# Attention stage of a fused attention and expert kernel: doubled result buffers, spread finish, earlier score groups, reordered start

## The chip, the cores and the metric

One core of a Trainium2 chip runs the program. The metric is device time in microseconds (us) of one execution; the kernel before takes 804.73 us, the median of 3 runs from 804.46 to 804.74. TensorE (PE) multiplies, VectorE (DVE), ScalarE (ACT) and GpSimd (POOL) work on tiles, SyncE (SP) issues transfers. Each engine works through its own instructions in the order in which the program has them.

## The reference

The computation is bucketed attention, then a gated product, then routed experts. The change touches the attention and the first of the gated products:

```python
q_bits = (np.einsum('bhsd,dk->bhsk', q, proj) > 0)     # 6 bits a row, k_bits likewise
mask = q_bucket[:, :, :, None] == k_bucket[:, :, None, :]
scores = np.where(mask, q @ k.T / sqrt(64), -1e9)      # 2 batches, 8 heads, 768 rows, 64 columns
attn = softmax(scores) ;  x = attn @ v                 # x: 1536 tokens x 512
x = (x @ w_a * (x @ w_b)) @ w_out                      # 512 -> 1536 -> 512, w in 64 bit
out = gate * relu(x @ w1[e]) @ w2[e]                   # one of 8 experts a token
```

## The kernel before

The attention works on eight pairs of heads (`i`). A pair has six **units** `u`, three a head, and a unit has two tiles of 128 query rows. All is in one loop over `u` from 0 to 49, in which each unit mixes the steps of several others:

- `scores(u, t)` (L161 to L172): four products into one of two score banks `st` (pool `ps_s`, two buffers). Half of them read swapped copies `qs`, `ks` of the transposed `q`, `k`, which SyncE makes (L127, L129).
- `rowmax` (L177) on VectorE, `expo` (L183) on ScalarE, which frees the score bank and sums; `recip` (L187), `normal` (L192 to L196) on GpSimd scales the exponentials; `turn` (L203) on VectorE transposes 32-blocks of unit `u - 2` into `et`.
- `pv` (L212): the product with `v`, 12 of a head's 24 blocks in a unit with `u % 3` of 0 or 1, into the four banks `pvb`. I call this a **product block**.
- in a unit with `u % 3 == 2` the four banks are read out and used for a later pair. `epilogue` (L230) copies them to `xp` and `co` on ScalarE. Then, where `u % 6 == 5` (a **turn unit**), `turned` (L107, L121) transposes the raw `q`, `k` of the pair after next, and where `u % 6 == 2` (a **sign unit**), `signs` (L139 to L152) makes the bucket codes `qf`, `kf` of the next pair (`sk` on the way).
- the **finish** of a pair, `xp + co` (L234, GpSimd), its high part `xh` (L238, ScalarE) and the rest `xl` (L242, GpSimd), stands at the ends of three units, `u % 6` of 5, 0 and 1. `xp` and `co` have one buffer each, so the `epilogue` of the next pair in the sign unit behind it writes the tiles that the finish reads.

The caller passes `hook`, with which steps of other work are placed at points of a unit: the weight splits (`load_first` for `w_a`, `w_b`, `w_out`: DVE steps L393, L396, L401, L415, ACT L409, L420, POOL L404, L421) by the table `places` and the list `tail`, and `fill`, which takes the first 16 half products of the gated stage (`gated_products`, L490, six matmuls each, copy `a` L498, product L502, cast L503) into units 41, 44, 47 to 49 and behind the loop. Behind the attention stands the gated stage, which begins with `yp` (L516).

Of the kernel before, what the change touches and what calls it, by code (L numbers as in the profile page):

```python
# [25 lines left out]
class Kernel:  # L26
# [37 lines left out]
    def attention(self, xh, xl, pools, hook):  # L64
# [9 lines left out]
        for tag, shape, dt, n in (  # L74
            ("et", [128, NC * S], F32, 2), ("e", [128, S], F32, 6), ("vr", [128, NC * 256], F32, 2), ("raw", [128, 2 * S], F32, 2),
            ("q", [128, S], F32, 2), ("qs", [128, S], F32, 2), ("k", [128, S], F32, 2), ("ks", [128, H2], F32, 2),
            ("xp", [128, S], F32, 1), ("co", [128, S], F32, 1), ("qf", [128, S], BF16, 2), ("kf", [128, S], BF16, 2), ("sk", [128, H2], BF16, 1),
        ):
            sb.tile(shape, dt, tag=tag, name=tag, bufs=n)
        raw, Q, QS, K, KS, QF, KF, VR = {}, {}, {}, {}, {}, {}, {}, {}  # L80

        def load(i, qs=(nc.sync, nc.sync)):
            b, hp = pairs[i]
            t = raw[i] = sb.tile([128, 2, NC, 2, D], F32, tag="raw", name="raw", bufs=2)
# [48 lines left out]
        def signs(i, n):  # L133
# [15 lines left out]
            def out():  # L149
                nc.scalar.activation(sk, p[:, 0, :H2], AF.Sign, bias=self.bias, scale=2.0 ** 100)  # L150
                for j in range(2):
                    nc.gpsimd.tensor_scalar(KF[i][:, j], sk, self.fac[:, j:j + 1], None, ALU.mult)  # L152
# [69 lines left out]
        def place(i, n, j, cs):  # L222
            if i not in XP:
                XP[i] = [sb.tile([128, S], F32, tag=t, name=t, bufs=1) for t in ("xp", "co")]
# [24 lines left out]
        hook(-1, 0)  # L249
        load(1)  # L250
        load_v(0)
        load_v(1)
# [9 lines left out]
        signs(0, 1)()  # L262
        signs(0, 0)()

        for u in range(NU + 2):
# [3 lines left out]
            done = (u - 11) // 6 if u >= 11 else -1  # L269
            fin = (u - 11) % 6  # L270
            if act:
                scores(u, 0)
                rowmax(u, 0)
            if s == 2 and u >= 8:
                for n in range(2):
                    epilogue((u - 8) // 3, n)
            if tr:
                turn(w, 0)
            if act:
                scores(u, 1)  # L280
                expo(u, 0)
            if last:
                recip(u - 1)
                normal(u - 1)
            hook(u, 3)
# [4 lines left out]
            preps = []  # L290
            if s == 2:
                n = (u + 7) // 6 if r == 5 else i + 1
                if u < NU and n < len(pairs):
                    preps = [(turned if r == 5 else signs)(n, x) for x in (1, 0)]
            elif u >= 6:
                pv((u - 6) // 3, range(12 * s, 12 * s + 12))
            if u == 0:
                n = 1
                preps = [turned(1, x) for x in (1, 0)]
            hook(u, 0)  # L300
            args = (nc.scalar,) if r in (5, 0) else ()
# [906 lines left out]
```

## Time and profile before

| | us |
|---|---|
| median of 3 runs | 804.73 |
| the profiled execution, its own time | 800.47 |
| its span on the core | 798.6 |
| TensorE busy | 727.9 (91%) |
| VectorE, GpSimd, ScalarE busy | 468.8, 458.8, 343.7 |

The page gives one execution. A share of busy time is a mean over stages with different limits: the attention stage fills the first 300 us or so of the span, and the rest is nearly all TensorE. What a change in the attention is worth is read from the waits of that stage and from the granted clock of its stretches (1.00 is 2.4 GHz, 0.5 is 1.2 GHz).

### The profile page before, as it was taken

The page shows a single profiled execution, that of the slowest core. Times are in us where ns is not written, and L with a number is a line of the kernel's source. Part 1 is how long each engine was busy: PE and PEld are TensorE (multiplying, and loading weights), DVE is VectorE, ACT ScalarE, POOL GpSimd, SP SyncE. Part 2 cuts the span into 40 slices and gives each one's busy share as a digit, 9 for nine tenths or more (in the row PEclk, how much of TensorE's full clock was granted, in tenths as well). Part 3 has the DMA queues.
Part 4 walks back from the last instruction along what each step waited for, and adds up shares of the span by engine and source line. Part 5 has one row for each costly group of instructions (what it writes and reads, how often), then busy time and mean ns, then how long its engine had stood idle before and what let it go on. Part 6 is the DMA issues. An engine that isn't in the chain of part 4 may idle for free.

```text
span 798.6 us, 16431 instructions
## 1 busy us (share of the span) xinstructions
PE 727.9 (91%) x6832; PEld 602.6 (75%) x6832; DVE 468.8 (59%) x679; ACT 343.7 (43%) x609; POOL 458.8 (57%) x468
## 2 busy tenths in 40 slices
PE   4788687798788789999999999999999999999996
PEld 3345354454456578999999999999999888899985
DVE  1499697786764826465465654643564665656551
ACT  1466466575653523421222212223353655555551
POOL 1387777787865654636356363555351575666651
PEclk9799999899997999999999999999999999999999
DMA  9433453542413131312113111144343376666620
GB/s 215 94 79 93 117 123 88 119 97 55 110 41 94 41 107 54 106 33 74 54 55 105 44 62 53 53 149 156 93 133 116 118 255 227 220 217 217 223 76 22
DMA packets 67485, 87.62 MB, mean 110 GB/s; under 512 B 28739, under 2 KB 40003, under 8 KB 67408
## 3 DMA queue, kind: packets, MB, share of 16 engines
q1 hardware_dynamic: 63200, 78.81, 34.3%
q0 software_dynamic: 2560, 7.34, 2.4%
q8 instruction: 54, 0.88, 0.5%
q10 hardware_dynamic: 1648, 0.39, 0.3%
q14 instruction: 23, 0.19, 0.1%
HBM read 75.52 MB, written 7.34 MB: 104 GB/s over the span
## 4 chain that ended last, share of the span: by engine, by line
PE 72%; POOL 8%; ACT 7%; DVE 5%; issue 4%; DMA 2%; SPq 1%; POOLq 0%; ACTq 0%; DVEq 0%
PE ab L490 23%; PE yp L516 12%; PE op L833 10%; PE hp L783 9%; PE st L170 3%; PE pv L212 3%; POOL e L196 3%; ACT e L183 3%; DVE nm L177 2%; PE pv L490 2%; POOL xl L242 2%; DVE et L203 2%; PE pv L139 2%; PE hr L801 1%; ACT co L230 1%
## 5 line engine op out<-in xcount | busy, mean ns | idle before, releaser
L490 PE MATMUL ab<-xh,w 128*128 128x384 f32 x704 | 185.7, 338 | 0.0
L177 DVE TENSOR_REDUCE nm<-st 128x1 f32<-128x768 f32 x96 | 90.7, 945 | 65.8 <-PE st L172 65.7
L490 PEld LDWEIGHTS ab<-xh,w 128*128 128x128 f32 x704 | 127.7, 188 | 0.8
L490 PE MATMUL ab<-xl,w 128*128 128x384 f32 x352 | 118.3, 336 | 0.0
L504 POOL TENSOR_TENSOR g<-a,g 128x384 fp32r<-128x384 f32 x48 | 50.0, 1042 | 114.1 <-ACT g L503 107.8
L739 POOL TENSOR_TENSOR w<-raw,w 128x1024 fp32r<-128x1024 f32 x36 | 88.1, 2450 | 36.7 <-ACT w L738 35.7
L183 ACT ACTIVATE e<-st,nm 128x768 f32<-128x768 f32 x96 | 86.2, 898 | 46.4 <-DVE nm L177 40.5
L516 PE MATMUL yp<-w,g 128*128 128x512 f32 x432 | 103.3, 391 | 0.8 <-DVE xp L335 0.8
L170 PE MATMUL st<-ks,qs 64*128 64x384 f32 x192 | 89.4, 547 | 15.4 <-DMA qs<-q 8.3
L196 POOL TENSOR_SCALAR e<-e,s,mc 128x768 f32<-128x768 f32 x96 | 96.5, 1012 | 5.3
L170 PE MATMUL st<-k,q 64*128 64x384 f32 x192 | 88.7, 543 | 10.7 <-ACT e L183 10.7
L203 DVE STREAM_TRANSPOSE et<-e 128x768 f32<-128x768 f32 x96 | 92.6, 965 | 0.0
L516 PEld LDWEIGHTS yp<-w,g 128*128 128x128 f32 x432 | 80.3, 188 | 16.3 <-PE yp L516 1.2
L833 PE MATMUL op<-w,hth 128*128 128x512 f32 x256 | 81.7, 400 | 0.0
L783 PE MATMUL hp<-xgh,w 128*128 128x256 f32 x448 | 80.6, 281 | 0.0
L212 PE MATMUL pv<-et,vr 32*64 32x192 f32 x3072 | 72.6, 331 | 4.5 <-ACT co L230 3.8
L212 PEld LDWEIGHTS pv<-et,vr 32*64 32x64 f32 x3072 | 61.4, 133 | 19.1 <-issue 7.3
L503 ACT CAST g<-a 128x384 fp32r<-128x384 f32 x48 | 24.7, 515 | 115.0 <-DVE a L502 115.0
L739 DVE TENSOR_TENSOR w<-raw,w 128x1024 fp32r<-128x1024 f32 x28 | 64.6, 2306 | 14.6 <-ACT w L738 14.3
L783 PEld LDWEIGHTS hp<-xgh,w 128*128 128x128 f32 x448 | 69.2, 188 | 0.3
L738 ACT CAST w<-raw 128x1024 fp32r<-128x1024 f32 x64 | 66.1, 1044 | 3.5 <-PE yp L516 3.5
L490 PEld LDWEIGHTS ab<-xl,w 128*128 128x128 f32 x352 | 66.2, 188 | 0.8
(189 smaller groups left out, 1217.5 us busy)
## 6 DMA issues: line engine op xcount, KB each, us to landing
raw<-in_moe_w_dram SPq DMA_DIRECT2D x32, 1024.0 KB, 5.7
vr<-in_v_dram SPq DMA_DIRECT2D x64, 192.0 KB, 4.2
raw<-in_moe_w_a_dram SPq DMA_DIRECT2D x5, 1024.0 KB, 5.0
raw<-in_moe_w_b_dram SPq DMA_DIRECT2D x5, 1024.0 KB, 5.1
raw<-in_moe_w_out_dram SPq DMA_DIRECT2D x5, 1024.0 KB, 5.0
raw<-in_k_dram SPq DMA_DIRECT2D x16, 192.0 KB, 5.3
qs<-q SPq DMA_DIRECT2D x16, 192.0 KB, 3.1
ybuf<-y SPq DMA_DIRECT2D x12, 256.0 KB, 6.2
```

The source lines that it names most:

```text
L170: nc.tensor.matmul(st[:, n, :H2], q[d, ql], k[d], start=True, stop=False, tile_position=(64 * n, 0))
L177: nc.vector.tensor_reduce(NM[u][:, t:t + 1], ST[u, t][:, :, :H2], axis=AX.XY, op=ALU.max, negate=True)
L183: nc.scalar.activation(e, ST.pop((u, t))[:, :, :H2], AF.Exp, bias=NM[u][:, t:t + 1], accum_out=SU[u][:, t:t + 1])
L196: nc.gpsimd.tensor_scalar(E[u, t], E[u, t], r[:, t:t + 1], c[:, t:t + 1], ALU.mult, ALU.add)
L203: nc.vector.transpose(ET[h][:, :, c], E.pop((u, t)).rearrange("p a (b s) -> p (a b) s", s=32))
L212: nc.tensor.matmul(pvb[m:m + 64, a, :NC * 32], v[d], et[d, n].rearrange("p c s -> p (c s)"), start=(n < 2), stop=(n >= NB32 - 2), tile_pos ...
L490: nc.tensor.matmul(p[:, :384], w[:, k, fs], x[:, k, cols], start=(k == 0 and n == 0), stop=(k == self.KD - 1 and n == 2),)
L516: nc.tensor.matmul(p, g[:, f, rows], w[:, f], start=(n == 0), stop=(n == 5))
L738: nc.scalar.copy(h, raw)
L739: eng.tensor_tensor(l, raw, f32(h), ALU.subtract)
L783: nc.tensor.matmul(p[:, :256], w[:, k, fs], x[:, k], start=(n == 0), stop=(n == 3 * self.KD - 1))
L833: nc.tensor.matmul(p, h[:, 2 * n + f, rows], w[:, f], start=(n == 0 and f == 0 and m == 0), stop=(n == 3 and f == 1 and m == 2),)
```

## The change

It makes these edits:

- `xp` and `co` get two buffers, `raw` one instead of two.
- The finish of a pair is spread over `u % 6` of 0 to 3: additions in two units, one cast `xh` of 768 columns in the sign unit, `xl` there and in the next. The last pair but one has another split.
- `scores(0, 0)` stands ahead of the loop, and a unit issues `scores(u, 1)` and `scores(u + 1, 0)` instead of `scores(u, 0)` and `scores(u, 1)`. `epilogue` follows the first `expo` instead of preceding it; both copies of `turned` and `signs` follow the second `expo` instead of enclosing it.
- At the start the second pair's load, the first weights and `v` are issued behind the swapped copies, the first `kf` is made on VectorE, and the second pair's `turned` and `signs` go to units 1 and 3.
- The splits of `w_out` go from the end (`tail`) to units 39 to 49, and the fills become 2 halves each at units 41, 44, 47 and the first hook behind the loop, and 8 at the end of the stage.

```diff
-            ..., ("raw", [128, 2 * S], F32, 2),
+            ..., ("raw", [128, 2 * S], F32, 1),
-            ("xp", [128, S], F32, 1), ("co", [128, S], F32, 1), ...
+            ("xp", [128, S], F32, 2), ("co", [128, S], F32, 2), ...
...
-        hook(-1, 0)
-        load(1)
-        load_v(0)
-        load_v(1)
...
         high[0](nc.scalar)
         high[1](nc.vector)
-        signs(0, 1)()
+        load(1)
+        hook(-1, 0)
+        load_v(0)
+        load_v(1)
+        signs(0, 1)(nc.vector)
         signs(0, 0)()
+        scores(0, 0)
...
+            if u == 1 or s == 2 and r == 5:
+                new = 1 if u == 1 else (u + 7) // 6
+                kind = turned
+            elif u == 3 or s == 2 and u > 2:
+                new = 1 if u == 3 else i + 1
+                kind = signs
             if act:
-                scores(u, 0)
                 rowmax(u, 0)
+                scores(u, 1)
+                expo(u, 0)
             if s == 2 and u >= 8:
                 for n in range(2):
                     epilogue((u - 8) // 3, n)
-            if tr:
-                turn(w, 0)
-            if act:
-                scores(u, 1)
-                expo(u, 0)
+            if u + 1 < NU:
+                scores(u + 1, 0)
             if last:
                 recip(u - 1)
                 normal(u - 1)
+            if tr:
+                turn(w, 0)
...
-            if preps:
-                preps[0](*args)
             if act:
                 expo(u, 1)
-            if preps:
-                preps[1](*args)
+            for prep in preps:
+                prep(*((nc.scalar,) if kind is turned else ()))
...
+            elif 0 <= done:
+                if fin in (1, 2):
+                    for g in ((0, 1), (2,))[fin - 1]:
+                        finish_add(done, cols[g])
+                if fin == 3:
+                    finish_high(done, slice(0, S))
+                if fin in (3, 4):
+                    for g in ((0, 1), (2,))[fin - 3]:
+                        finish_low(done, cols[g])
...
+                (39, 39, 40, 41, 41, 41, 42), (45, 46, 46, 47, 47, 48, 49),
...
-            fill = {41: 4, 44: 4, 47: 2, 48: 2, 49: 2, NU + 2: 2}
+            fill = {41: 2, 44: 2, 47: 2, NU + 2: 2, NU + 3: 8}
```

On SyncE at the program's start, before (loads of the second pair, weights and `v`, then the swapped copies `ks`, `qs` of the first pair):

```order
L248 DMA pr<-in_proj_dram 64x6
L388 DMA spare<-in_moe_w_a_dram 128x4x256
L388 DMA spare<-in_moe_w_b_dram 128x4x256
L87 DMA raw<-in_k_dram 128x6x64
L87 DMA raw<-in_q_dram 128x6x64
L87 DMA raw<-in_k_dram 128x6x64
L87 DMA raw<-in_q_dram 128x6x64
L94 DMA vr<-in_v_dram 32x4x384 x8
L129 DMA ks<-k 64x384 x2
L127 DMA qs<-q 64x768 x2
```

And after:

```order
L248 DMA pr<-in_proj_dram 64x6
L129 DMA ks<-k 64x384 x2
L127 DMA qs<-q 64x768 x2
L87 DMA raw<-in_k_dram 128x6x64
L87 DMA raw<-in_q_dram 128x6x64
L87 DMA raw<-in_k_dram 128x6x64
L87 DMA raw<-in_q_dram 128x6x64
L391 DMA spare<-in_moe_w_a_dram 128x4x256
L391 DMA spare<-in_moe_w_b_dram 128x4x256
L94 DMA vr<-in_v_dram 32x4x384 x8
```

The four swapped copies moved ahead of fourteen loads.

On ScalarE from unit 11's end to the units behind sign unit 14, before (`e` are exponentials):

```order
L238 CAST xh_98<-xp 128x256
L183 ACTIVATE e,su<-st,nm 128x768
L420 CAST w<-spare 128x4x128
L183 ACTIVATE e,su<-st,nm 128x768
L238 CAST xh_98<-xp 128x256 x2
L183 ACTIVATE e,su<-st,nm 128x768 x2
L230 COPY xp<-pv 64x4x6x32
L230 COPY co<-pv 64x4x6x32
L183 ACTIVATE e,su<-st,nm 128x768
L150 ACTIVATE sk<-pv,bias 128x384
L183 ACTIVATE e,su<-st,nm 128x768
L140 ACTIVATE qf<-pv,bias 128x768
```

And after, from unit 12 on:

```order
L423 CAST w<-spare 128x4x128
L412 ACTIVATE spare<-spare 128x512
L183 ACTIVATE e,su<-st,nm 128x768 x4
L230 COPY xp<-pv 64x4x6x32
L230 COPY co<-pv 64x4x6x32
L183 ACTIVATE e,su<-st,nm 128x768
L150 ACTIVATE sk<-pv,bias 128x384
L140 ACTIVATE qf<-pv,bias 128x768
L238 CAST xh_98<-xp 128x768
L183 ACTIVATE e,su<-st,nm 128x768 x5
```

The three casts of 256 columns became one of 768 behind `qf`; the first exponential of the sign unit moved ahead of the copies `xp`, `co`, the second ahead of `sk`.

## Rows read from the trace of the kernel before

**Rows 1.** The page: TensorE's busy tenths in 40 slices, and a DMA issue.

```profile
PE   4788687798788789999999999999999999999996
...
qs<-q SPq DMA_DIRECT2D x16, 192.0 KB, 3.1
```

**Rows 2.** Waits of TensorE: line <- releaser: us in total, times, longest.

```profile
PE pv L145 <- ACT co L230: 17.6, 6, 3.7
```

**Rows 3.** Waits of ScalarE, same columns.

```profile
ACT xp L230 <- POOL xl L242: 20.4, 7, 3.2
ACT xh L238 <- POOL xp L234: 18.8, 18, 3.5
```

**Rows 4.** Six sign crossings: stretch, length, busy by engine, PEclk, DMA share, GB/s.

```profile
58.05:67.19 9.14, 8.39 (x137) 4.39 (x129) 8.06 (x13) 6.96 (x14) 7.60 (x13) 1.00 0.35 92
...
211.79:224.04 12.25, 8.57 (x136) 4.34 (x128) 8.05 (x11) 7.52 (x14) 9.74 (x16) 1.00 0.28 66
sum 79.73, PE 56.71 PEld 28.04 DVE 49.38 ACT 45.86 POOL 60.64; mean PE 9.45 PEld 4.67 DVE 8.23 ACT 7.64 POOL 10.11
```

**Rows 5.** Five turn crossings, their sum.

```profile
sum 45.66, PE 39.07 PEld 23.79 DVE 43.15 ACT 39.75 POOL 38.10; mean PE 7.81 PEld 4.76 DVE 8.63 ACT 7.95 POOL 7.62
```

**Rows 6.** Plain units 7 and 10, same columns as rows 4.

```profile
53.65:58.05 4.40, 4.23 (x117) 2.66 (x109) 4.28 (x7) 2.43 (x5) 4.04 (x7) 1.00 0.89 193
67.19:71.14 3.95, 3.95 (x117) 2.72 (x109) 3.40 (x6) 1.17 (x4) 3.38 (x6) 1.00 0.02 4
```

**Rows 7.** Units 41 and 42, 44 and 45, and unit 47 to `yp`.

```profile
227.99:241.26 13.27, 11.00 (x152) 7.55 (x144) 8.72 (x12) 7.70 (x15) 7.71 (x14) 1.00 0.27 61
245.21:264.69 19.48, 14.74 (x152) 10.96 (x145) 8.71 (x12) 7.38 (x14) 9.58 (x16) 0.74 0.33 95
268.64:298.97 30.33, 23.30 (x453) 19.84 (x445) 16.07 (x22) 11.31 (x21) 19.75 (x24) 0.89 0.31 97
```

**Rows 8.** Timeline of ScalarE, sign unit 8: start, us, what, idle before it.

```profile
59.29 0.80 ACT L230 COPY co<-pv 64x768 f32<-64x768 f32 x1
...
62.53 0.58 ACT L150 ACTIVATE sk<-pv,bias 128x384 bf16<-128x384 f32 x1 [1.32 <-PE pv L139]
...
63.88 0.90 ACT L140 ACTIVATE qf<-pv,bias 128x768 bf16<-128x768 f32 x1
```

**Rows 9.** Timeline of TensorE, sign unit 8 and the next block.

```profile
60.14 0.87 PE L145 MATMUL pv<-k,lz 128*64 128x384 f32 x4 [0.20 <-ACT co L230]
60.93 1.56 PE L139 MATMUL pv<-q,lz 128*128 128x384 f32 x4
...
65.05 2.21 PE L212 MATMUL pv<-et,vr 32*64 32x192 f32 x96
```

**Rows 10.** Timeline of TensorE, turn unit 23.

```profile
138.53 1.53 PE L107 MATMUL pv<-ident,raw 128*128 128x128 f32 x12 [0.54 <-ACT co L230]
```

**Rows 11.** Timeline of SyncE at the start.

```profile
16.42 1.30 SPq L127 DMA_DIRECT2D qs<-q  x2
```

**Rows 12.** Timeline of VectorE at the start.

```profile
9.33 0.96 DVE L123 TENSOR_SCALAR q<-pv 128x768 f32<-128x768 f32 x1 [1.65 <-ACT k L121]
24.68 0.96 DVE L177 TENSOR_REDUCE nm<-st 128x1 f32<-128x768 f32 x1 [14.40 <-PE st L172]
```

**Rows 13.** Chain of work that ended last: start, us, what.

```profile
228.00 0.99 ACT e L183 x2
...
230.68 2.37 PE pv L490 x12
...
250.41 4.22 PE pv L490 x12
```

**Rows 14.** The casts `xh`, L238: ns shortest, median, longest, and shapes.

```profile
L238 ACT CAST xh<-xp x23: 404/405/512, 78.2 to 301.3; 128x256 fp32r<-128x256 f32 x21, 128x384 fp32r<-128x384 f32 x2
```

**Rows 15.** The additions of the finish, L234, same columns.

```profile
L234 POOL TENSOR_TENSOR xp<-xp,co x21: 719/728/1163, 77.3 to 285.8; 128x256 f32<-128x256 f32 x21
```

**Rows 16.** A step of the weight splits on VectorE, same columns.

```profile
L396 DVE SCALAR_TENSOR_TENSOR spare<-spare x4: 780/1274/1276, 45.9 to 149.7; 128x512 int32<-128x512 int32 x4
```

More of the change, by code (lines that the diff above doesn't have):

```diff
@@ L289, in attention @@
                 turn(w, 1)
[L290 to L295, printed above, removed]
+            if new < len(pairs):
+                preps = [kind(new, x) for x in (1, 0)]
+            elif s < 2 and u >= 6:
                 pv((u - 6) // 3, range(12 * s, 12 * s + 12))
-            if u == 0:
-                n = 1
-                preps = [turned(1, x) for x in (1, 0)]
             hook(u, 0)
-            args = (nc.scalar,) if r in (5, 0) else ()
-            if preps:
-                preps[0](*args)
             if act:
                 expo(u, 1)
-            if preps:
-                preps[1](*args)
-            if preps and r in (5, 0) and n + 1 < len(pairs):
-                load(n + 1)
+            for prep in preps:
+                prep(*((nc.scalar,) if kind is turned else ()))
+            if preps and kind is turned and new + 1 < len(pairs):
+                load(new + 1)
             if s == 1 and u >= 7 and (u - 1) // 3 < 2 * len(pairs):
@@ L982, in late @@
             def late():
-                return sb.tile([128, 2 * S], F32, tag="raw", name="late", bufs=2)
+                return sb.tile([128, 2 * S], F32, tag="raw", name="late", bufs=1)
             jobs = [X.load_first(w, f, spare) for f in range(2) for w in range(2)]
             outs = [X.load_first(2, f, late) for f in range(2)]
-            plan = {(-1, 0): [jobs[0][0], jobs[1][0]], (NU - 5, 1): [j[0] for j in outs]}
+            plan = {(-1, 0): [jobs[0][0], jobs[1][0]], (36, 1): [outs[0][0]], (43, 1): [outs[1][0]]}
             places = (
                 (3, 4, 5, 6, 6, 9, 12), (7, 10, 11, 12, 12, 13, 18), (15, 17, 19, 22, 22, 23, 28), (21, 25, 26, 28, 28, 29, 34),
+                (39, 39, 40, 41, 41, 41, 42), (45, 46, 46, 47, 47, 48, 49),
             )
-            for (_, steps), us in zip(jobs, places):
+            for (_, steps), us in zip(jobs + outs, places):
                 for m, u in enumerate(us):
@@ L996, in tile_kernel @@
             plan[13, 0], plan[19, 0] = [jobs[2][0]], [jobs[3][0]]
-            r, o = [j[1] for j in outs]
-            def both(*steps):
-                return lambda: [step() for step in steps]
-            tail = [r[0], r[1], both(*r[2:5]), o[0], o[1], r[5], both(*o[2:5]), r[6], o[5], o[6]]
             first = [(t, f, w, h) for t in range(2) for f in range(2) for w in range(2) for h in range(2)]
-            fill = {41: 4, 44: 4, 47: 2, 48: 2, 49: 2, NU + 2: 2}
+            fill = {41: 2, 44: 2, 47: 2, NU + 2: 2, NU + 3: 8}
             def hook(u, at):
@@ L1010, in hook @@
                     job()
-                if u >= NU - 2 and at in (0, 1, 3) and tail:
-                    tail.pop(0)()
                 if at == 0:
@@ L1016, in hook @@
                         if half == 0:
-                            X.part = K.banks[:, n // 2] if u < NU else K.bank()
+                            X.part = K.banks[:, (2 if u == 44 else 0) + n // 2] if u < NU else K.bank()
                         X.gated_products(0, t, f, w, half, X.part)
             K.attention(X.xh, X.xl, (sb, ps_s, ps_pv), hook)
-            assert not plan and not first and not tail
+            assert not plan and not first
         pctx = ExitStack()
```

30 lines of the change are left out of this document (13 added, 17 removed).

## Prediction

> **What bounds the kernel now.** I read the page's slices first. TensorE is nearly full from the 16th slice of 20 us on [rows 1], which is the stage of the gated products and experts; the change does not touch what stands there, so that stage keeps its length. What can move is the attention stage, from the first row maximum at 24.68 us [rows 12] to the first output product `yp`, which starts after 298.97 us [rows 7]. There I asked for the waits. TensorE stands six times, 17.6 us in all, until ScalarE has copied a finished head (`co`) out of the bank that it needs [rows 2]; ScalarE in turn waits for GpSimd's `xl` before it may write `xp` again, and for GpSimd's additions before the casts `xh` [rows 3]. So I cut the stage at the product blocks (`pv`, 12 of 24 pieces of one head) on TensorE, and measured from the end of one block to the end of the next. There are three kinds of stretch.
>
> A plain unit (two scores, one block) takes 3.95 us with TensorE full, 4.40 us where a DVE step of a weight split stands ahead [rows 6]. A turn crossing (the unit with `turned` and the next one) takes 45.66 / 5 = 9.13 us [rows 5]. A sign crossing (the unit with `signs` and the next one) takes 9.14 us where no earlier pair is being finished, and 79.73 us over all six, with 12.25 in the last [rows 4]. The difference to 9.14 us is the wait of `xp` for `xl`, seven times [rows 3], and what half clock follows it. Two larger holes are the stretches with fills at units 41 and 44, 13.27 and 19.48 us, and the last one, 30.33 us from the end of unit 46's block to `yp` [rows 7].
>
> **The change, part by part.** I walk the new order with the durations of the rows, times counted from the end of a block (0). From the plain unit, a score group is (3.95 - 2.21) / 2, about 0.9 us [rows 6, 9]; an exponential with its sum is 0.99 us [rows 13], a reduction 0.96 us [rows 12].
>
> *Doubled `xp` and `co`, finish spread.* The wait of rows 3 goes: the copies of a new pair write other buffers, and additions end a unit before the cast asks for them (two at 0.73 us and one [rows 15], behind normalisations). What is late next is the new order itself. The first score group of the next unit now stands on TensorE ahead of the block, and needs the exponential of its own bank; ScalarE has both prep copies, and in sign units a 768-column cast, ahead of it.
>
> Sign crossing: exponential until 1.0; two copies of 0.80 until 2.6 [rows 8]; sign products 0.87 and 1.56 until 4.95 [rows 9], while the second exponential is hidden; `sk` 0.58 and `qf` 0.90 until 6.4 [rows 8]; the cast of 768 columns until 7.2 (256 columns are 0.41 us, 384 are 0.51 [rows 14], so I take 0.8, between 0.51 and three times 0.41); the next exponential until 8.2; score group 9.1; block 11.3. Without the cast, in the first pair, 10.5. Six give 10.5 + 5 x 11.3 = 67.0 against 79.7: **-12.7**. So the clean 9.14 us is not reached: before, the block waited for the second exponential alone.
>
> Turn crossing: 1.0, 2.6, transposes 1.53 until 4.15 [rows 10], two copies (0.8 each by the nearest row [rows 8]) until 5.7, exponential 6.65, scores 7.55, block 9.7. Five times 9.7 against 45.7: **+2.8**.
>
> *Fills.* At unit 41 two halves (2.37 us [rows 13]) instead of four: 2.6 + 2.37 = 5.0, copy 0.5 (as a 384-column cast [rows 14]), two exponentials until 7.45, scores, block 10.5, against 13.27: **-2.8**. At unit 44: 5.0, product and cast 0.5 each, exponential 7.05, cast `xh` 7.85, exponential 8.8, scores and block 11.9, against 19.48, which ran at a mean clock of 0.74 [rows 7]: **-7.6**.
>
> *The end.* From unit 46's block: fill until 5.0, the blocks of units 48 and 49 directly behind it until 9.3, one fill until 11.4 (4.22 us at half clock [rows 13], so 2.11 back to back at the full one). On the other side the last exponential ends at 6.5, the normalisation takes two times about 1 us (like a reduction [rows 12]) and small steps until about 9, three additions [rows 15] until 11.1, cast 11.5, two copies 13.1; the last head's two blocks until 17.4; eight halves, four times 2.11, until 25.8. They cover the last finish (copies and casts of 384 columns, some 0.5 each [rows 14], and as many on VectorE). Before it was 30.33: **-4.5**. All sixteen halves are done at that point in both.
>
> *Start.* The swapped copies `ks`, `qs` now stand ahead of second pair, weights and `vr` on SyncE. Before, `qs` was issued at 16.42 us [rows 11] and the first maximum came at 24.68 us after 14.40 us of idle VectorE [rows 12]. Now they go out when `q` is written at 10.3 us [rows 12]: issue 1.30 [rows 11], landing 3.1 (the median of its kind [rows 1]) gives about 14.5, first maximum 15.3. `kf` moves from GpSimd to VectorE, idle there; no row shows it, its bounds are 0 and two times 0.96, both hidden behind the landing. Behind the copies on SyncE are queued the second pair's loads; its transposes move to unit 1, about 21 us, so they are bounded by 0 and some 3 us of wait. Following units 0 to 5 in the same way (about 4 us each, two crossings among them without blocks) brings the first block's end to 45.3 us against 53.65 [rows 6]: **-8.4**, with 5 and 10 as ends.
>
> *Weight splits on VectorE.* A step behind the second transpose now delays the next reduction, exponential and the score group ahead of the block; before only two units showed it (4.40 us [rows 6]). Fourteen such steps from unit 7 on, 0.45 (rows 6) to 1.27 us each (`top`, [rows 16]); I take 0.5, since a part of them meets slack: **+7.0**, between 0 and 14.
>
> *Clock.* In the new crossings TensorE waits about 2.3 us (5.9 to 8.2) in one place. Rows show both: 12.25 us with a longer wait at clock 1.00 [rows 4], and 0.74 [rows 7]. A spell costs 1.85: the same twelve products took 2.37 and 4.22 us [rows 13]. I take two, **+3.7**, between 0 and 24 (thirteen such waits: six sign, five turn, two fill).
>
> *`raw` in one buffer.* Its load still stands behind the transposes that free it, six units ahead of its use: nothing; the cover is some 25 us of work.
>
> Sum: -12.7 + 2.8 - 2.8 - 7.6 - 4.5 - 8.4 + 7.0 + 3.7 = -22.5 us. The profiled run is 800.47 us (span 798.6 and 1.87 around it), so 778.0 us there; the median 804.73 lies 4.26 us above it, which gives **782.2 us**.
>
> **The rivals.** (a) *Half clock at every returning wait.* The waits of TensorE come back in each crossing, small but regular. Then the clock term is 24 and not 3.7: -2.2, 802.5 us. Against it: the first sign crossing has 0.75 us idle and the last one over 3.6, both at 1.00 [rows 4]. The Trainium skill (TensorE: Matmul & The Clock Gate, "A second HAM failure mode: psum-queue depth-cycling") says that cycling through PSUM banks with frequent small idle times makes the gate swing between its two rates; by that rule the kernel would come out near that time. Rows 4 bear it out only in part.
>
> (b) *The wait stays.* The casts `xh` still wait for the additions [rows 3], and if GpSimd is late in the sign unit, ScalarE stands there instead of at `xp`: 12.7 goes to nothing, 794.9 us.
>
> (c) *Slower.* The place is the score group ahead of the block in plain units. The loop over two units is score group 0.9, reduction 0.96, transpose (taken as long as a reduction) 0.96, reduction 0.96, exponential 0.99, score group 0.9, block 2.21: 7.88 us, 3.94 a unit beside 3.95 of TensorE's own work, so no slack. If GpSimd's normalisation comes late, the transposes wait and each unit pays. From 0.5 us a unit in all 46 units it outweighs 22.5 us; at 0.8 us the time is 782.2 + 37 = 819 us. Against it: by the walk, normalised tiles are ready some 2 us before the transposes ask.
>
> (d) *More gain.* Split steps and clock cost nothing, and the crossings run as the clean ones did (12.2 less in the sign, 2.8 less in the turn ones): -22.5 - 7.0 - 3.7 - 15.0 = -48, 757 us. Against it: ScalarE's order, in which the exponential stands last.
>
> **How the numbers follow.** Forecast 0.68, (a) 0.07, (b) 0.09, (c) 0.07, (d) 0.09. The forecast's own terms (start 3, splits 7, clock 5, crossings 5) give 771 to 793; to hold 8 in 10 I reach a little to (b) and (d): 768 to 795. A measurement here can tell about 0.2%, 1.6 us. (a) counts half as faster; with the rest: faster 0.89, same 0.03, slower 0.08.
>
> **What would show it.** Right: no row of `xp` waiting for `xl`; sign crossings of 11 to 11.5 us with TensorE idle in front of a score group released by an exponential; turn crossings of about 9.7; first maximum near 15.3; TensorE without a hole behind the last head. Wrong: plain units above 4.2 us, a clock under 0.9 over the attention stage, `xh` waits as long as before, or transposes of the second pair waiting for `raw`.

## The result

The changed kernel takes 782.01 us (median of 4 runs, 778.43 to 782.81), beside 804.74 us for the kernel before; the ratio is 0.9704, 95% interval 0.9669 to 0.9738. The prediction was 782.2 us, between 768 and 795. The profiled execution of after is 781.45 us with a span of 779.7; before it was 800.47 and 798.6, so the two traces differ by 18.9 us, and it is these 18.9 us that the traces can account for.

The page of after, busy tenths of TensorE in 40 slices, answers [rows 1]: the nearly full slices begin one slice earlier, at the fifteenth.

```profile
PE   6788888887887899999999999999999999999996
```

Waits of TensorE in after (line <- releaser: us in total, times, longest) answer [rows 2]. The wait for `co` has gone from 17.6 us to 2.5; in its place the score groups wait for exponentials, 35.5 us in all.

```profile
PE st L170 <- ACT e L183: 35.5, 27, 2.3
...
PE pv L145 <- ACT co L230: 2.5, 6, 0.4
```

In before the score groups' wait was half as long:

```profile
PE st L170 <- ACT e L183: 17.7, 24, 2.3
```

Waits of ScalarE in after answer [rows 3]: `xh` waits 0.6 us in all, not 18.8, and no row of `xp` waiting for `xl` is left.

```profile
ACT xh L238 <- POOL xp L234: 0.6, 2, 0.3
ACT xp L230 <- PE pv L212: 0.3, 1, 0.3
```

The stretches of after, cut at the same points as [rows 4 to 7] (columns as there: length, then busy time by engine, then the granted clock, DMA share and GB/s). First the sign crossings: the first, which has no cast, the fifth, and the sum of six.

```profile
49.33:60.31 10.98, 8.66 (x137) 4.34 (x129) 8.48 (x14) 7.58 (x14) 6.57 (x10) 1.00 0.28 74
...
171.60:184.29 12.69, 10.21 (x137) 5.48 (x129) 8.36 (x11) 8.78 (x16) 9.15 (x14) 0.87 0.26 64
...
sum 76.25, PE 59.95 PEld 31.74 DVE 54.58 ACT 51.31 POOL 53.75; mean PE 9.99 PEld 5.29 DVE 9.10 ACT 8.55 POOL 8.96
```

The sum of the five turn crossings, and that of the fourteen plain units:

```profile
sum 49.64, PE 39.27 PEld 24.48 DVE 43.65 ACT 40.53 POOL 42.45; mean PE 7.85 PEld 4.90 DVE 8.73 ACT 8.11 POOL 8.49
```

```profile
sum 55.43, PE 55.43 PEld 37.97 DVE 40.96 ACT 15.49 POOL 48.62; mean PE 3.96 PEld 2.71 DVE 2.93 ACT 1.11 POOL 3.47
```

Units 41 and 42, 44 and 45, and from unit 46's block to `yp`:

```profile
218.69:229.52 10.83, 8.60 (x141) 5.63 (x133) 8.47 (x14) 7.14 (x14) 8.64 (x14) 1.00 0.32 74
233.58:246.82 13.24, 10.01 (x141) 6.16 (x133) 9.24 (x13) 7.41 (x14) 9.43 (x17) 0.87 0.41 101
250.77:280.32 29.55, 24.28 (x470) 21.47 (x463) 13.11 (x20) 12.04 (x23) 14.19 (x19) 0.94 0.33 100
```

Put side by side, in us (the plain units of before are what the other stretches leave of 298.97):

| stretch | before | after | difference | predicted |
|---|---|---|---|---|
| start to the first block's end | 53.65 | 45.38 | -8.3 | -8.4 |
| six sign crossings | 79.73 | 76.25 | -3.5 | -12.7 |
| five turn crossings | 45.66 | 49.64 | +4.0 | +2.8 |
| fourteen plain units | 56.85 | 55.43 | -1.4 | +7.0 |
| units 41, 42 | 13.27 | 10.83 | -2.4 | -2.8 |
| units 44, 45 | 19.48 | 13.24 | -6.2 | -7.6 |
| unit 46's block to `yp` | 30.33 | 29.55 | -0.8 | -4.5 |
| `yp` to the end | 499.6 | 499.4 | -0.2 | 0 |
| half clock, not placed | | | in the rows above | +3.7 |
| sum | | | -18.9 | -22.5 |

Where a sign crossing loses its time is seen in unit 26. The timeline of TensorE (start, us, what, idle before it), with the sign products, the early score group and the block:

```profile
174.08 0.87 PE L145 MATMUL pv<-k,lz 128*64 128x384 f32 x4 [0.41 <-ACT co L230]
174.88 1.56 PE L139 MATMUL pv<-q,lz 128*128 128x384 f32 x4
...
179.51 0.59 PE L170 MATMUL st<-ks,qs 64*128 64x384 f32 x1 [2.07 <-ACT e L183]
...
180.52 3.84 PE L212 MATMUL pv<-et,vr 32*64 32x192 f32 x96
```

And ScalarE there:

```profile
176.47 0.58 ACT L150 ACTIVATE sk<-pv,bias 128x384 bf16<-128x384 f32 x1 [1.43 <-PE pv L139]
176.95 0.90 ACT L140 ACTIVATE qf<-pv,bias 128x768 bf16<-128x768 f32 x1
177.73 0.83 ACT L238 CAST xh<-xp 128x768 fp32r<-128x768 f32 x1
178.46 0.91 ACT L183 ACTIVATE e<-st,nm 128x768 f32<-128x768 f32 x1
```

The early score group of unit 27 stands 2.07 us for the exponential that ScalarE reaches behind `sk`, `qf` and the cast, as the walk had it. But the block behind it, 2.21 us in [rows 9], takes 3.84: most of it runs at half clock, as the stretch of its first 1.5 us shows.

```profile
180.50:182.00 1.50, 1.50 (x42) 1.28 (x48) 1.03 (x2) 0.32 (x1) 1.20 (x4) 0.50 0.00 0
```

That is 1.63 us, and the granted clock is 0.87 in this crossing and in the four others that have a cast, and 1.00 in the first. All five stand 2.07 us ahead of the early group, the first 1.34 us.

### The profile page after: what moved, and what is told of

Same layout as the page of the kernel before. It is cut to its first block, busy times and chain, and to the rows that moved or that the text cites. A ratio compares the mean times of both kernels' runs of the same rounds, so it can differ in the third digit from the quotient of the medians.

```text
span 779.7 us, 16454 instructions
## 1 busy us (share of the span) xinstructions
PE 720.6 (92%) x6832; PEld 599.8 (77%) x6832; DVE 463.6 (59%) x681; ACT 342.4 (44%) x597; POOL 457.6 (59%) x466
## 4 chain that ended last, share of the span: by engine, by line
PE 78%; ACT 8%; DVE 5%; issue 4%; POOL 3%; DMA 1%; SPq 0%; POOLq 0%; ACTq 0%; DVEq 0%
PE ab L493 22%; PE yp L519 12%; PE op L836 10%; PE hp L786 9%; PE pv L212 8%; PE st L170 5%; ACT e L183 3%; DVE nm L177 2%; PE pv L139 2%; PE hr L804 2%; PE part L493 1%; PE lgp L602 1%; DVE et L203 1%; ACT co L230 1%; PE pv L493 1%
## 5 line engine op out<-in xcount | busy, mean ns | idle before, releaser
L507 POOL TENSOR_TENSOR g<-a,g 128x384 fp32r<-128x384 f32 x48 | 54.8, 1141 | 114.5 <-ACT g L506 105.1
L170 PE MATMUL st<-ks,qs 64*128 64x384 f32 x192 | 86.3, 530 | 20.8 <-ACT e L183 20.8
L170 PE MATMUL st<-k,q 64*128 64x384 f32 x192 | 86.5, 531 | 14.8 <-ACT e L183 14.7
L212 PE MATMUL pv<-et,vr 32*64 32x192 f32 x3072 | 79.4, 354 | 2.0 <-issue 1.5
L212 PEld LDWEIGHTS pv<-et,vr 32*64 32x64 f32 x3072 | 66.2, 145 | 19.5 <-issue 14.4
```

Of the source, the lines that this page charges most:

```text
L170: nc.tensor.matmul(st[:, n, :H2], q[d, ql], k[d], start=True, stop=False, tile_position=(64 * n, 0))
L212: nc.tensor.matmul(pvb[m:m + 64, a, :NC * 32], v[d], et[d, n].rearrange("p c s -> p (c s)"), start=(n < 2), stop=(n >= NB32 - 2), tile_pos ...
```

## The experiments

Each kernel was run beside the kernel before. A crossing is always cut as in [rows 4, 5]; the time of a whole kernel is a median.

**The order put back.** The units of after in the order of before; everything else of the change stays.

```diff
-        scores(0, 0)
...
             if act:
+                scores(u, 0)
                 rowmax(u, 0)
-                scores(u, 1)
-                expo(u, 0)
             if s == 2 and u >= 8:
                 for n in range(2):
                     epilogue((u - 8) // 3, n)
-            if u + 1 < NU:
-                scores(u + 1, 0)
+            if tr:
+                turn(w, 0)
+            if act:
+                scores(u, 1)
+                expo(u, 0)
...
-            if tr:
-                turn(w, 0)
...
+            args = (nc.scalar,) if preps and kind is turned else ()
+            if preps:
+                preps[0](*args)
             if act:
                 expo(u, 1)
-            for prep in preps:
-                prep(*((nc.scalar,) if kind is turned else ()))
+            if preps:
+                preps[1](*args)
```

> The changed kernel, with the order inside a unit put back as before: scores(u, 0) and scores(u, 1) in one unit, the copies xp and co ahead of the first exponential, the two prep copies around the second one. Doubled buffers, spread finish, start and fills stay. Theory (the doubling gains, the new order gives part of it back, because the product block waits for an exponential behind all prep copies): sign crossings fall from 12.7 to 13.6 us to about 9.2, turn crossings from 9.8 to 9.1, no wait of TensorE over 1 us there, so no half clock: 6 x 3.6 + 5 x 0.7 = 25 us less, about 756 us. Rival (the earlier score groups are what gains, since plain units now hold 3.95 us with weight splits beside them): plain units with splits go back to 4.4, crossings stay over 11 us, 785 us or more.

Measured: 757.75 us (757.23 to 758.28), ratio 0.9413 (0.9379 to 0.9448), 24.3 us less than after. The six sign crossings of this kernel:

```profile
sum 56.37, PE 51.05 PEld 26.21 DVE 49.57 ACT 45.80 POOL 51.30; mean PE 8.51 PEld 4.37 DVE 8.26 ACT 7.63 POOL 8.55
```

19.9 us less than after's, all at clock 1.00, and that is most of the difference. Not all got shorter: the plain units are 2.7 us longer (58.10), as the rival had it in part, since four of them take 4.48 to 5.16 us; and the turn crossings, expected at 9.1 us, take 10.19 in the mean, one of them 12.51 at a clock of 0.86. The timeline of TensorE in the same unit shows why the sign crossings are shorter:

```profile
164.48 0.59 PE L170 MATMUL st<-ks,qs 64*128 64x384 f32 x1 [0.55 <-ACT e L183]
...
165.49 2.21 PE L212 MATMUL pv<-et,vr 32*64 32x192 f32 x96
```

Ahead of the block only the two groups of its own unit stand. Both need exponentials of the sign unit, the second of which ScalarE now runs between `sk` and `qf`; the wait is 0.55 us. In after a third group stands there and needs an exponential of the next unit. So the new order of the units loses what the doubled buffers win.

**The doubling alone.** The kernel before with two `xp` and `co`, one `raw`, its second pair's load behind the transposes, and the `w_out` splits where after has them; order, finish, fills and start are those of before.

```diff
-            ..., ("raw", [128, 2 * S], F32, 2), ("xp", [128, S], F32, 1), ("co", [128, S], F32, 1), ...
+            ..., ("raw", [128, 2 * S], F32, 1), ("xp", [128, S], F32, 2), ("co", [128, S], F32, 2), ...
...
-        load(1)
...
         high = turned(0, 1), turned(0, 0)
+        load(1)
         high[0](nc.scalar)
         high[1](nc.vector)
...
```

> The kernel before with doubled xp and co alone, and what the room for them forces: raw in one buffer, the second pair's load behind the first transposes, the w_out splits at the new units. Old order, old finish, old fills, swapped copies behind the loads. Theory: the wait of xp for xl is the whole of the excess in sign crossings, so these go from 79.7 us in sum to about 57, units 44 and 47 lose 3 us each: 804.7 - 23 - 6 = about 776 us, faster than the changed kernel although less is changed. Rival (the spread of the finish is needed: additions late on GpSimd keep the casts xh waiting and ScalarE with them): sign crossings stay over 11.5 us, 793 us or more.

Measured: 768.83 us, ratio 0.9565 (0.9525 to 0.9604), 7 us less than expected. Its sign crossings, then units 44 and 45 and the end:

```profile
sum 56.36, PE 50.93 PEld 26.09 DVE 48.02 ACT 43.12 POOL 52.64; mean PE 8.49 PEld 4.35 DVE 8.00 ACT 7.19 POOL 8.77
```

```profile
227.64:240.61 12.97, 10.85 (x145) 7.56 (x145) 8.23 (x13) 7.15 (x14) 9.85 (x16) 1.00 0.42 103
244.56:266.58 22.02, 20.59 (x453) 16.84 (x445) 12.54 (x17) 10.23 (x19) 17.13 (x22) 1.00 0.44 133
```

The crossings fall from 79.73 to 56.36 us: the wait of [rows 3] and the half clock behind it were nearly the whole excess over 9.14 us a crossing. Units 44 and 45 fall from 19.48 to 12.97 and the end from 30.33 to 22.02; in those two the moved `w_out` splits can have a part, which no run separates. This version is 13 us faster than the full change, although it lacks the new start, whose price follows below.

**Products into the wait.** After, with twelve small products more in each unit behind a sign unit, ahead of the early score group. They add work and take none away.

```diff
+            if act and u % 6 == 3 and u > 3:
+                for m in range(12):
+                    nc.tensor.transpose(pvb[:, 3, m % 4 * 128:m % 4 * 128 + 128], self.ident, self.ident)
```

> The changed kernel with twelve 128x128 transposes of the identity added on TensorE in the unit behind each sign unit (seven times), where it waits some 2 us for an exponential; their result is overwritten by the product block and used nowhere. Theory (each such wait brings a half-clock spell that doubles the product block behind it, 3.84 instead of 2.21 us): no spell there, the block at 2.21, 6 or 7 times 1.6 = about 10 us less, 772 us. Rival (spells come by themselves, or the added work delays more than it saves): spells stay, 782 us or up to 784.

Measured: 779.14 us, ratio 0.968 (0.9641 to 0.9719), not the 772 expected. That interval overlaps after's, so the whole time decides little; the sign crossings, the fifth and the sum of six, decide:

```profile
170.47:181.51 11.04, 10.09 (x149) 5.63 (x141) 7.38 (x10) 8.24 (x16) 8.84 (x15) 1.00 0.30 75
...
sum 68.62, PE 60.88 PEld 33.78 DVE 50.56 ACT 48.59 POOL 48.10; mean PE 10.15 PEld 5.63 DVE 8.43 ACT 8.10 POOL 8.02
```

More work, 7.6 us less time: all six run at clock 1.00. The other stretches together were longer in this trace by 5.6 us (start 2.0, end 1.75, units 41 and 42 1.2, turn crossings 1.1, units 44 and 45 0.5 shorter), and so most of the gain was paid back. The start has a mean clock of 0.93 there and 1.00 in after, the end 0.89 and 0.94; for the rest the trace names no cause.

**The copies behind the loads.** After with the swapped copies behind the loads again; unlike in before, the second pair's load stands ahead of the weights.

```diff
-        high[0](nc.scalar)
-        high[1](nc.vector)
         load(1)
         hook(-1, 0)
         load_v(0)
         load_v(1)
+        high[0](nc.scalar)
+        high[1](nc.vector)
```

> The changed kernel with the swapped copies of the first pair behind the loads of the second pair, of the weights and of v again. Theory: first row maximum at 24 to 26 us instead of 14.7, and the whole 8 to 10 us stay to the end: 790 to 792 us. Rival (the lead is lost later, since the first product block needs six units and v in any case): under 785 us.

Measured: 795.55 us, ratio 0.9878 (0.984 to 0.9916), longer than either expectation; so the place of the copies is worth 13.5 us to this kernel, more than the 8.3 of the table. The timeline of VectorE has the first row maximum at

```profile
28.11 0.96 DVE L177 TENSOR_REDUCE nm<-st 128x1 f32<-128x768 f32 x1 [15.95 <-PE st L172]
```

That is later than the 24.68 of [rows 12], and the first block ends at 60.05 us instead of 45.38. SyncE's timeline names the difference to before:

```profile
8.15 0.54 SPq L87 DMA_DIRECT2D raw<-in_k_dram  x1
...
20.45 1.29 SPq L127 DMA_DIRECT2D qs<-q  x2
```

With one `raw` the second pair's load waits until 8.15 us for the transposes that free it, and weights, `v` and then `qs`, queued behind it, go out later, `qs` at 20.45 us instead of 16.42 [rows 11]. A single `raw` doesn't cost this by itself: in the doubling alone, where weights and `v` stand ahead of that load, the first row maximum comes at 24.84 us. From the first maximum to the first block's end it is 31.94 us here, 30.65 in after and 28.97 in before, but 26.51 with the order put back: the new order has a part in it.

**One half of the order put back, and the other.** First the score groups alone: both of a unit in that unit, ScalarE's order as in after. (The prep copies are the two copies that ScalarE makes in `turned` or `signs`. The expectations from here on call them swapped copies; `qs` and `ks` are not meant.)

```diff
-        scores(0, 0)
...
             if act:
+                scores(u, 0)
                 rowmax(u, 0)
...
-            if u + 1 < NU:
-                scores(u + 1, 0)
```

> After with one part of the unit order put back: both score groups of a unit are issued in that unit, ahead of its product block, instead of the first one a unit early; ScalarE keeps the order of after (epilogue behind the first exponential, swapped copies behind the second). Theory: a sign crossing costs 12.7 us in after because TensorE, which takes its work in order, stands 2.07 us at the second score group for the exponential ahead of it and then walks one spell at half clock; with the groups together both can be written as soon as their two tiles come free, the wait is under 2 us in two places instead of one, and the half-clock spells of the sign crossings go. Expected 768 to 772 us, sign crossings 10.5 to 10.9 us each, no spell at half clock in them. Rival: the place of ScalarE's epilogue and swapped copies alone makes the crossing long; then the time stays at 780 to 783 us with a spell in each crossing.

Measured: 795.84 us (788.02 to 798.48), ratio 0.9888 (0.9853 to 0.9924). Both expectations fall. Waits of TensorE:

```profile
PE pv L145 <- ACT co L230: 16.5, 6, 2.9
PE pv L107 <- ACT co L230: 13.0, 5, 3.2
```

The wait for `co` of [rows 2] is back, with another cause: the epilogue stands behind the first exponential, and that exponential now needs a row maximum whose scores were only just issued (this is read from the order of the code). Then ScalarE's order alone: the epilogue ahead of the first exponential and the prep copies around the second, the early group kept.

```diff
-                expo(u, 0)
             if s == 2 and u >= 8:
                 for n in range(2):
                     epilogue((u - 8) // 3, n)
+            if act:
+                expo(u, 0)
...
+            args = (nc.scalar,) if preps and kind is turned else ()
+            if preps:
+                preps[0](*args)
             if act:
                 expo(u, 1)
-            for prep in preps:
-                prep(*((nc.scalar,) if kind is turned else ()))
+            if preps:
+                preps[1](*args)
```

> After with the other part of the unit order put back: ScalarE's epilogue ahead of the first exponential, and the two swapped copies around the second one, as before; the score group of the next unit stays ahead of the block. With after (both new, 782.0), the version with both old (757.8) and the version with only the score groups old (795.8) it makes a table of two by two. Theory: what sets a sign crossing is that the early score group needs an exponential that ScalarE reaches only behind both sign copies and the cast, in either order of ScalarE's other work; so 775 to 785 us, with the wait of the early score group for that exponential still near 2 us. Rival: the order on ScalarE alone is the harm, and the time falls near that of both old, 756 to 762 us.

Measured: 822.68 us, ratio 1.0229 (1.0192 to 1.0266): longer than before, though the interval leaves open whether by 2%. Both expectations fall again. Waits of TensorE:

```profile
PE st L170 <- ACT e L183: 67.5, 49, 2.2
```

The early group, which stands ahead of the sign products, waits for an exponential behind the epilogue, and each sign crossing has two more such waits behind them. So the table of two by two reads 782.0 (both new), 795.8 and 822.7 (one of each), 757.8 (both old). The parts are not worth an amount each: an early group needs the early exponential, a late group needs the early epilogue. My reading that the early group alone did the harm fails in that form; what does it is the pair.

**The cast out of the sign unit.** After, with the 768-column cast and the subtractions one unit later.

```diff
-                if fin == 3:
+                if fin == 4:
                     finish_high(done, slice(0, S))
-                if fin in (3, 4):
-                    for g in ((0, 1), (2,))[fin - 3]:
+                if fin in (4, 5):
+                    for g in ((0, 1), (2,))[fin - 4]:
```

> After with the 768-column cast of a pair's finish moved one unit later, out of the unit with the sign work, and the subtractions that follow it one unit later as well. Theory: that cast stands on the path of the sign crossing (the first pair's, which has none, takes 10.98 us against 12.69 to 13.55 for the others, with a TensorE wait of 1.3 us and no half clock); without it each of the other five takes about 11 us. Expected 770 to 778 us. Rival: the cast lies beside other work and the spells come from the order of the units alone; then the time is 780 to 783 us.

Measured: 770.96 us (770.2 to 771.38), ratio 0.9603 (0.9579 to 0.9628), 11.0 us less than after and as expected. The fifth sign crossing on TensorE:

```profile
172.21 0.59 PE L170 MATMUL st<-ks,qs 64*128 64x384 f32 x1 [1.34 <-ACT e L183]
...
173.21 2.21 PE L212 MATMUL pv<-et,vr 32*64 32x192 f32 x96
```

and the sum of six:

```profile
sum 64.07, PE 51.60 PEld 26.08 DVE 50.47 ACT 47.72 POOL 46.97; mean PE 8.60 PEld 4.35 DVE 8.41 ACT 7.95 POOL 7.83
```

The wait falls from 2.07 to 1.34 us, and the block takes 2.21. The last five crossings mean 10.61 us against 13.05: 2.44, of which the cast is 0.83 and the half clock 1.63. One step of 0.83 us on ScalarE cost three times its length. The spells are not those of one execution: the mean granted clock of the whole run is 0.980 to 0.989 in the four runs of after and 0.991 to 0.995 in the four of this version.

**The block first.** After, with the early score group behind the block in the unit that follows a sign or turn unit.

```diff
-            if u + 1 < NU:
+            if u + 1 < NU and s:
                 scores(u + 1, 0)
...
                 pv((u - 6) // 3, range(12 * s, 12 * s + 12))
+            if u + 1 < NU and not s:
+                scores(u + 1, 0)
```

> After with one group moved: in the unit behind a sign or turn unit (the first of each head) the score group of the next unit is issued behind the product block instead of ahead of it; all else as in after. Theory: in after TensorE stands 2.07 us in front of that group while the block behind it could already run; with the block first it fills that wait. In sign unit 26 the block could then run from 177.9 us (end of qf) to 180.1, the early group until 181.0 and the following unit would be some 2.3 us earlier; over six crossings about 14 us, five turn crossings some 1 us each, and no half-clock spell in a sign crossing. Expected 760 to 768 us. Rival: the wait moves behind the block, since the next unit's group then waits for its exponential as long; 778 to 782 us.

Measured: 775.89 us, ratio 0.9645 (0.9621 to 0.967): between the two expectations, nearer to the rival. The sign crossings are at clock 1.00 and 49.93 us, but each of the fourteen stretches that were plain units now takes 6.36 us (a stretch, then the sum):

```profile
176.59:182.95 6.36, 5.03 (x122) 3.12 (x115) 4.35 (x6) 2.80 (x7) 5.63 (x12) 1.00 0.01 3
...
sum 89.33, PE 70.66 PEld 43.60 DVE 67.34 ACT 35.59 POOL 79.60; mean PE 5.05 PEld 3.11 DVE 4.81 ACT 2.54 POOL 5.69
```

Each of them has one score group more (about 1.1 us of TensorE) and, as in unit 28, a wait of about 1.3 us for the next exponential. Taken with the turn crossings (41.43), the three kinds come to 180.7 us against 181.3 in after, but they hold three groups more, since the start and the two fill crossings now end a group earlier: like for like they are some 3.8 us shorter. The waits didn't go: score groups stand 32.6 us for exponentials in all, and the blocks 6.3 us for the prep copies. So the wait moved by one unit, as the rival said; what went is the half clock, in the five crossings and in unit 44, and the 6 us gained are less than these spells cost in after.

**Both together.** The block first and the cast later (the two edits above).

> The same version (block first in the unit behind a sign or turn unit) with, in addition, the 768-column cast moved one unit later, out of the sign unit. Theory: with the block first the early group is no longer what the sign crossing waits for, so the cast stands beside other work, and the two changes do not add: 0 to 3 us less than with the block first alone, 758 to 766 us. Rival: they add, the cast's 11 us come off in full: 750 to 756 us.

Measured: 771.74 us, ratio 0.9592 (0.9568 to 0.9616). 4.2 us less than the block first alone and no better than the cast alone: they do not add. The difference of 0 to 3 us was estimated a little low (turn crossings fell by 4.4 us); the time, 758 to 766 us, was missed by 6 because it built on the block-first time that was expected.

**Three more on the old order.** The old order with both prep copies behind the second exponential; the same with the fills of before; the same with the cast later (the cast's edit is the one above).

```diff
-            args = (nc.scalar,) if preps and kind is turned else ()
-            if preps:
-                preps[0](*args)
             if act:
                 expo(u, 1)
-            if preps:
-                preps[1](*args)
+            for prep in preps:
+                prep(*((nc.scalar,) if kind is turned else ()))
```

> The version with the old unit order (757.75 us) with one thing kept from after: the two swapped copies of ScalarE both stand behind the second exponential, instead of one ahead of it and one behind. Theory: the copy ahead of the second exponential lies on the path of a crossing, about 0.7 us in each; behind both it lies beside VectorE's reductions. Expected 751 to 753 us, sign crossings 8.1 to 8.7 us, turn crossings 9.3 to 9.5 us. Rival: what is won at the exponential is lost at the next block, which waits for the copies; then 757 to 759 us.

```diff
-            fill = {41: 2, 44: 2, 47: 2, NU + 2: 2, NU + 3: 8}
+            fill = {41: 4, 44: 4, 47: 2, 48: 2, 49: 2, NU + 2: 2}
...
-                            X.part = K.banks[:, (2 if u == 44 else 0) + n // 2] if u < NU else K.bank()
+                            X.part = K.banks[:, n // 2] if u < NU else K.bank()
```

> The version before this one (old unit order, swapped copies behind both exponentials) with the output-product filling of the kernel before (four groups at units 41 and 44, two each at 47, 48, 49) in place of after's. Theory: the two units and the end take 48.5 us with the old filling against 50.0 with the new one (from the versions measured so far), so it is 1 to 2 us less than that version: 750 to 751 us. Rival: the filling is worth nothing by itself and the two times agree within 0.5 us, or the old filling delays units 41 and 44 more than the end gains, 2 us slower.

> The version with the old unit order and both swapped copies behind the second exponential (756.2 us) with the 768-column cast moved one unit later. Theory: in the old order the block waits for no exponential behind the cast; ScalarE has slack there and the time changes by less than 1.5 us: 754.7 to 757.5 us. Rival: the cast delays the next unit's first exponential and the reduction chain behind it; without it each sign crossing gains 0.5 us or more: 752 to 754 us.

Measured: 756.18 us (0.9428; 0.9399 to 0.9458), 757.51 (0.9435; 0.941 to 0.946) and 757.74 (0.9407; 0.9384 to 0.943). None can be told from the old order's 757.75, so the first two expectations are missed. The copies gave 3.4 us in the sign crossings (52.96) and the plain units took 1.2 back (59.30), 1.6 us in the median where I expected 5 to 7. The old fills made the end 23.49 us instead of 28.30 and units 41 to 45 27.57 instead of 20.83, where 1 to 2 us less in all was expected: half products moved, and no time was won. The cast, worth 11 us in after, is worth nothing here; in the timeline of the old order the block waits for an exponential that ScalarE runs ahead of the cast. All of these beat both kernels, after by 24 to 26 us and before by 46 to 48.

## Why the prediction was right, step by step

**The total.** It was right to 0.2 us, and part of that is luck. In the traces the change is -18.9 us and not -22.5. The profiled execution of before lay 4.3 us below its median, that of after 0.6 below its own, and this offset fills the gap. Within the sum, two wrong terms nearly cancelled: the splits (+7.0, where the plain units came out 1.4 us shorter) and the half clock (+3.7, about 10 came). The end, 3.7 us worse than said, and smaller terms leave the 3.6 us.

**The wait goes, and the new order takes most of it back.** Right. No `xp` waits for `xl`, `xh` waits 0.6 us, and TensorE stands in front of a score group released by an exponential. The walk gave 11.3 us with the cast and 10.5 without. Measured are 13.05 less 1.63 of half clock, 11.4, and 10.98; with the products in the wait, so with the clock held, they mean 11.44. The size of the sign term, -12.7, was missed almost by the clock alone: 76.25 less five times 1.63 is 68.1, against 67.0.

**Turn crossings**: walked 9.7, measured 9.81 in four and 10.41 in the first. Right.

**The clock term** is the step that failed: I took two spells at half clock. There were seven: one in each of the five sign crossings with a cast (about 1.6 us each: TensorE is busy 10.21 to 10.28 us there, 8.66 in the first), one in unit 44 (TensorE busy 10.01 us there, 8.60 in unit 41 with as many instructions) and one in the last fill (3.18 us for twelve products that took 2.37 in [rows 13]). Together that is 8.0 + 1.4 + 0.8 = 10.2. Rival (a) had the mechanism, and a price for thirteen waits that was too high: none of the five turn crossings, each with a wait of 1.48 us, lost its clock. What the Trainium skill (TensorE: Matmul & The Clock Gate, "A second HAM failure mode: psum-queue depth-cycling") tells of another kernel, that small idle times which keep coming back make the gate swing, agrees with five of the six sign crossings and with no turn crossing. In the experiment with the cast, 0.83 us less on ScalarE's path was enough to end it in the sign crossings.

**The weight splits** cost nothing in the plain units: fourteen of them take 55.43 us, 3.95 or 3.96 in all but one. The step let each of fourteen steps delay the next reduction by 0.5 us, and neither that nor the walk of rival (c), which found no slack, had been held against a row. The slack is there: in the plain units of after VectorE is busy 2.93 us of 3.96. It comes with the early group: in the old order put back, the four plain units that take 4.48 to 5.16 us have VectorE busy 4.26 to 5.16 us of it. Rival (c) falls with it.

**Start**: predicted 15.3 us for the first maximum and 45.3 for the first block's end. SyncE issues `qs` at 10.44, and VectorE's timeline has

```profile
11.78 0.55 DVE L152 TENSOR_SCALAR kf<-sk,fac 128x384 bf16<-128x384 bf16 x2 [1.67 <-ACT sk L150]
14.73 1.82 DVE L177 TENSOR_REDUCE nm<-st 128x1 f32<-128x768 f32 x2 [2.40 <-PE st L172]
```

14.73 and 45.38. Right, and `kf` on VectorE was hidden.

**Units 41 and 44**: -2.4 and -6.2 for -2.8 and -7.6; the rest of unit 44 is its half-clock spell.

**The end** was over-estimated: -0.8 for -4.5. The last exponential ended at 258.94, 8.2 us behind unit 46's block and not 6.5, and the last head's blocks begin at 16.1 instead of 13.1. VectorE and ScalarE there, then TensorE:

```profile
249.70 0.65 DVE L399 SCALAR_TENSOR_TENSOR late<-late 128x512 int32<-128x512 int32 x1
250.27 0.42 DVE L404 TENSOR_SCALAR r<-late 128x512 int32<-128x512 uint32 x1
250.60 0.95 DVE L177 TENSOR_REDUCE nm<-st 128x1 f32<-128x768 f32 x1
...
260.79 1.29 DVE L418 SCALAR_TENSOR_TENSOR late<-late 128x512 f32<-128x512 f32 x1
262.01 1.82 DVE L203 STREAM_TRANSPOSE et<-e 128x768 f32<-128x768 f32 x2
```

```profile
257.57 0.48 ACT L501 COPY a<-pv 128x384 f32<-128x384 f32 x1 [2.56 <-PE pv L493]
257.94 0.91 ACT L183 ACTIVATE e<-st,nm 128x768 f32<-128x768 f32 x1
```

```profile
263.80 0.88 PE L212 MATMUL pv<-et,vr 32*64 32x192 f32 x23 [1.48 <-issue]
```

The two split steps hold the first of unit 47's row maxima back by about 1 us, here where there is no slack, and the last exponential stands on ScalarE behind the fill's copy `a`, which waits for the fill at half clock, 0.8 us more. These two make up the 1.7 us: by the walk's own durations a fill until 5.0, a copy of 0.5 and an exponential of 0.99 end at 6.5. Then TensorE stands another 1.48 us, which the walk had at nothing, until the transposes behind a third split step (L418) end, and the last blocks follow. All this is read from the trace; no run took the steps away.

**The rivals.** (b) fell with the `xh` row. (d), 757 us, is about the time that the old order of the units gives (757.75), though not by (d)'s sum: its trace is 42.1 us shorter than that of before and not 48, and the offset of before's execution fills this gap too. Sign crossings of 9.39 us in the mean were to be had, and the new order, which I had named against it, kept them away; the turn crossings were 10.19 and not 9.13.

## What to carry to other kernels

Before work is issued earlier on an in-order engine, ask what it needs and where that stands on the other engine's list: a group moved ahead of a block that could run makes the block wait for everything ahead of the group's own input. Two orders that are each other's condition are tested together, since one of them alone can be slower than either pair. Price a wait of TensorE by its length and by the clock behind it, and where a wait comes back in every round, count a spell for each round until a row says otherwise.

## What the runs showed of the hardware

The granted clock hangs on little. With waits of 2.07 us in five sign crossings the block behind them ran at half clock, with 1.34 us at the full one, in the same program but for the place of one cast. Yet the length of one wait alone doesn't settle it. In before, five sign crossings stand 3.13 to 3.68 us for `co`; two of them have a clock of 1.00 and three of 0.77 to 0.90. The clearest pair is units 44 and 45 of the block first and of both together: the same instructions at the same distances for 6.5 us, with the same wait of 2.28 us at their end, and behind it a block at clock 1.00 in the one (the first two lines) and at 0.55 in the other (the last two):

```profile
235.54 0.59 PE L170 MATMUL st<-ks,qs 64*128 64x384 f32 x1 [2.28 <-ACT e L183]
...
236.55 2.21 PE L212 MATMUL pv<-et,vr 32*64 32x192 f32 x96
```

```profile
229.93 0.59 PE L170 MATMUL st<-ks,qs 64*128 64x384 f32 x1 [2.28 <-ACT e L183]
...
230.94 3.85 PE L212 MATMUL pv<-et,vr 32*64 32x192 f32 x96
```

And in the version with ScalarE's old order a turn crossing, which takes 11.97 us with TensorE busy 7.91, stands twice for 1.78 us around its transposes and keeps its clock, as do three of the other four; the fifth has 0.87:

```profile
187.29 0.59 PE L170 MATMUL st<-k,q 64*128 64x384 f32 x1 [1.78 <-ACT e L183]
...
188.37 1.53 PE L107 MATMUL pv<-ident,raw 128*128 128x128 f32 x12
191.68 0.59 PE L170 MATMUL st<-k,q 64*128 64x384 f32 x1 [1.78 <-ACT e L183]
```

What tells the stretches that lose the clock from those that keep it the runs leave open.
